# Attention with the row maxima first: how the first rows of maxima reach the queries, and where the last lead products stand

## The chip, the cores and the metric

The kernel runs on one core of one Trainium2 chip. Its engines work side by side and meet only at semaphores: TensorE (PE, with its weight loads PEld shown apart), VectorE (DVE), ScalarE (ACT), GpSimd (POOL) and the sync engine SP, which here only issues transfers. The metric is the device time of one execution in microseconds (us). Three runs of the kernel before took 1555.54, 1555.70 and 1554.82 us, median 1555.54.

## The reference

One transformer block on 2048 rows of 512 numbers: a modulated layer norm, attention with 32 query heads of 16 numbers on one shared key and value head, an output projection, a gate and a residual, then a second modulated layer norm and a two-layer network with gelu.

```
mod = (silu(c) @ w_mod)                     # six rows of 512: sa, ca, ga, sb, cb, gb
h = layernorm(x) * (1 + ca) + sa
q = (h @ wq), 32 heads of 16;  k = h @ wk;  v = h @ wv      # one k and one v for all heads
scores = q . k * 16 ** -0.5
p = softmax(scores);  o = p @ v;  x = x + ga * (o @ wo)
h = layernorm(x) * (1 + cb) + sb
x = x + gb * (gelu(h @ w1 + b1) @ w2 + b2)
```

## The kernel before

**Attention in units.** The 2048 rows are cut into eight blocks of 256, the 32 heads into eight groups of four: 64 units. A unit goes through two passes over all 2048 keys. The first takes maxima: a score product `m` (L512; 128 queries against 512 keys on one half of the array's rows) goes to a PSUM bank and VectorE reduces it to one maximum for each query (L517, `mx`). A unit has 32 such products, and 64 units have 2048. The second pass computes the scores again, now with keys as rows (`e`, L617), and ScalarE takes the exponential into SBUF (`p`, L621); then `acc` (L638) multiplies with the values.

**Where the maxima go.** A softmax needs the maximum subtracted before the exponential. The kernel lets the array do that: the operand tiles `qst` have two rows in each half, 48 and 49 (and 112 and 113), that hold the maximum's high and low part, against rows of `ks` that are -1. So no `e` of a unit can start before its maxima stand in those rows. The way there is `put_max`: VectorE reduces `mx` to `mm` (128 queries x 8) and turns it in 32x32 squares (`turned`), GpSimd gathers the four bands into `mt` (8 x 128, L560), splits that into a high and a low part `mh` and `ml` (L133, L140), and transfers write them into `qst` (L555), one for each part and half.

**The start.** Ahead of the loop over units stands a stretch with an order of its own, the table `SLOTS`: each entry takes a number of score products (`chunk`) and then names pieces of other work, such as the key projections ("keys"), the last query projection ("q 1", tile `qps`), turning the values into place ("v 2", "v 3", tile `vps`), preparing query weights ("wq"), and four pieces of modulation rows ("rows", tile `modl`). The score products in it belong to the units 0 and 1, alternately for the lower and upper half of the array. Their PSUM banks are a ring of three (tag `m`): a product can start when the product three before it in the ring has been reduced. PSUM has three more banks for exponentials (`e0` to `e2`), one for `x` and one for `v`.

**The lead.** After the table the score products must have reached a given count ahead of the exponentials, `lead[0]`, which is 56: all 32 of unit 0 and 24 of unit 1. Then `keep_warm` issues products whose result nobody reads, so that TensorE has work while the first rows travel. Then the loop begins. It goes in half steps, each ending with an `acc` group of eight products (16 in the profile's count); in a half step four `e` and, as a rule, four `m` are mixed, and in most of them a batch of other products (projections, the network) in between. The number of `m` in a step comes from `lead`, so a product that is not made before the loop is made in its first step. In the function `plain`, used for the first step, one `m` of each half step is put into bank `x`.

The order on each engine is exactly the order in which the program issues.

Of the kernel before, what the change touches and what calls it, by code (L numbers as in the profile page):

```python
# [8 lines left out]
F32 = mybir.dt.float32  # L9
# [5 lines left out]
P = 128  # L15
# [5 lines left out]

LEAD = 6
LEAD_0 = 6
FIRST_MAX = ((0, 0), (1, 0), (0, 1), (1, 1), (0, 2), (0, 3), (1, 2), (1, 3))
SLOTS = ((2, "keys 1", "keys 1"), (2, "keys 1", "keys 1"), (2, "low 1", "heads 2"), (2, "heads 2", "k 1"), (1, "warm"), (1, "heads 2"), (2, "heads 2", "v 0"),
# [4 lines left out]
MAX_WAIT = (1, 4)  # L30
QBUFS = 4
PREP = 4
# [9 lines left out]
SOON = 6  # L42
GROUP = 4
NORM_WAIT = 6
WARM = (4, 16, 2, 5)
MOD_WAIT = 3
AHEAD = 4.5

# [1 line left out]
def raw(ap):  # L50
    return ap.bitcast(F32)
# [3 lines left out]
def adaln_mqa_mlp(  # L55
# [15 lines left out]
    nc = tc.nc  # L71
# [22 lines left out]
    att = ctx.enter_context(tc.tile_pool(name="att", bufs=1))  # L94
    psum = ctx.enter_context(tc.tile_pool(name="psum", bufs=1, space=bass.MemoryType.PSUM))

    def pad(pool, nbytes, name):

        nc.gpsimd.memset(pool.tile([P, nbytes // 4], F32, name=name), 0.0)
# [27 lines left out]
    def ebank():  # L127
        turns[0] += 1
        return dict(tag=f"e{turns[0] % 3}", bufs=1)

    def split(dst_h, dst_l, src, eng_h, eng_l, between=None):
        if eng_h is nc.gpsimd:
            eng_h.tensor_scalar(out=dst_h, in0=src, scalar1=1.0, scalar2=0.0, op0=ALU.mult, op1=ALU.add)  # L133
        elif eng_h is nc.scalar:
            eng_h.copy(dst_h, src)
        else:
            eng_h.tensor_copy(out=dst_h, in_=src)
        if between:
            between()
        eng_l.tensor_tensor(out=dst_l, in0=src, in1=raw(dst_h), op=ALU.subtract)  # L140
# [7 lines left out]
    def later(n, fn):  # L148
        if draining[0]:
            fn()  # L150
        else:
            pending.append((clock[0] + n, fn))
# [130 lines left out]

    idles = []

    def keep_warm(n, **place):

        for k in range(n):
            if k == 0 or not place:
                ps = psum.tile([P, BQ], F32, name=f"idle{len(idles)}", **(place or dict(tag="m", bufs=3)))  # L290
                idles.append(ps)
            nc.tensor.matmul(ps, wkH[:, 0, :], wkH.rearrange("p k n -> p (k n)"), start=True, stop=True)

    def mod_rows(ps, k, wm):

# [19 lines left out]
    wkH = pro.tile([P, KD, P], F32R, name="wkH")  # L315
# [32 lines left out]
    bigH = att.tile([P, NB - 1, KD, BQ], F32R, name="bigH", tag="bigH")  # L348
# [8 lines left out]
    def stats1(b, between=None):  # L357
        mv, rs = ln_stats(xts[b], pro, QT, between)
        nm = pro.tile([P, QT], F32, name=f"nm{b}", tag="nm", bufs=2)
        if b:  # L360
            nc.gpsimd.tensor_tensor(out=nm, in0=mv[:, :, 0], in1=rs, op=ALU.mult)
            nc.gpsimd.tensor_scalar(out=nm, in0=nm, scalar1=-1.0, scalar2=0.0, op0=ALU.mult, op1=ALU.add)
        hts_stats[b] = mv, rs, nm

    def xhat1(b, eng):

        mv, rs, nm = hts_stats[b]
        xt = xts[b]
# [118 lines left out]
    class Max:  # L487


        def __init__(self):  # L490
            def products(u, kcs):
                return [(u, j, t, kc) for kc in kcs for j in range(2) for t in range(blocks[units[u][0]][1] // P)]

            def in_rows(u):
                return [(u, j, t, kc) for j in range(2) for t in range(blocks[units[u][0]][1] // P) for kc in range(NKC)]


            begin = [o for u, kc in FIRST_MAX for o in products(u, [kc])]
            self.todo = [begin + [o for u in range(2, NU) for o in in_rows(u)] for _ in range(2)]
# [30 lines left out]
    placed = set()  # L530
# [5 lines left out]
    def put_max(u, mx):  # L536

        T = blocks[units[u][0]][1] // P  # L540
        qst = qsts[u]
        mm = mms[u % 2]
        turned = att.tile([P, 32], F32, name=f"turned{u}", tag="turned", bufs=2)
        if u == 0:
            pad(att, 256, "pad7")
        mt = att.tile([4 * T, P], F32, name=f"mt{u}", tag="mt", bufs=2)
        mh = att.tile([4 * T, P], F32R, name=f"mh{u}", tag="mh", bufs=2)
        ml = att.tile([4 * T, P], F32R, name=f"ml{u}", tag="ml", bufs=2)

        def send():  # L550
            for s in range(2):
                for r, src in ((48, mh), (49, ml)):
                    dst = qst[64 * s + r:64 * s + r + 1].rearrange("p j (t n) -> p (j t) n", n=P)
                    ring = nc.scalar if u == 0 and s else nc.sync
                    ring.dma_start(out=raw(dst), in_=raw(src[2 * T * s:2 * T * (s + 1), :].unsqueeze(1)))  # L555
            placed.add(u)

        def gather():
            for g in range(0, P, 32):
                nc.gpsimd.tensor_scalar(out=mt[:, g:g + 32], in0=turned[g:g + 4 * T, :], scalar1=1.0, scalar2=0.0,  # L560
                                        op0=ALU.mult, op1=ALU.add)
            split(mh, ml, mt, nc.gpsimd, nc.gpsimd)

        def reduce():
            nc.vector.tensor_reduce(out=mm[:, :4 * T], in_=mx, axis=AX.X, op=ALU.max)
            nc.vector.transpose(out=turned, in_=mm)  # L566
            later(MAX_WAIT[0], gather)
            later(MAX_WAIT[1], send)


        if NQ <= u < NQ + 2:
            reduce()
        else:
            later((0 - clock[0]) % 4 + 1, reduce)
# [661 lines left out]
    first = [sum(size[:u]) for u in range(NU + 1)]  # L1236
    mp = Max()

    def chunk(n):
        for _ in range(n):  # L1240
            mp.step(mp.done % 2)

    act, dve, pool = nc.scalar, nc.vector, nc.gpsimd

# [50 lines left out]
    def warm():  # L1295
        keep_warm(WARM[2], tag="x")
        yield
# [16 lines left out]
    mod1(0, 0, act, pool)  # L1314
    turn1(0, 3)
    keep_warm(WARM[0])
    mod1(0, 1, pool, dve, lambda: stats1(1))
    load_constants()
    mod1(0, 2, act, dve)
    mod1(0, 3, act, dve)  # L1320
    rows = xhat1(1, act)
# [17 lines left out]
    def last_h(t):  # L1339
        if t == QT - 1:  # L1340
# [6 lines left out]
    run(xhat1(3, pool))  # L1347
    keep_warm(WARM[1])
    work = {"keys 1": keys(1), "heads 2": heads(2), "heads 3": heads(3), "q 1": q_group(), "keys 2": keys(2), "keys 3": keys(3),
            "v 0": one(v_out, 0), "v 1": one(v_out, 1), "v 2": one(v_out, 2), "v 3": one(v_out, 3), "rows": late_rows(),  # L1350
            "low 1": one(low_k, 1), "low 2": one(low_k, 2), "low 3": one(low_k, 3), "k 1": one(repeat_k, 1), "k 2": one(repeat_k, 2), "k 3": one(repeat_k, 3), "load": one(load_q, 2), "warm": warm(),
            "wq 1": one(prep_wq, 1), "wq 2": one(prep_wq, 2), "wq 3": one(prep_wq, 3)}
    for n, *names in SLOTS:
        chunk(n)
        for name in names:
            next(work[name])
    assert 0 in placed and len(mods_late) == KD
    draining[0] = False
    nc.gpsimd.tensor_scalar(out=b1r, in0=b1c, scalar1=GELU_R, scalar2=0.0, op0=ALU.mult, op1=ALU.add)
# [8 lines left out]
    lead = [first[u + 1] + 4 * LEAD for u in range(NU)] + [first[NU] + 4 * LEAD]  # L1368
    for u in range(NQ):
        lead[u] = min(first[1] + 4 * LEAD_0 + (lead[NQ] - first[1] - 4 * LEAD_0) * u / NQ, first[u + QBUFS - 1] - 2)  # L1370

# [1 line left out]

        return sum(b_.shape[-1] * (4 if b_.dtype == F32 else 1) for _, _, b_, _, _ in batch) / 512

    while mp.done < lead[0]:
        chunk(1)
    preps["w1"] = prep_w1()
    w2H = w2L = None
# [27 lines left out]
            if units[u][1] == NQ - 1:  # L1407
                put_off(rest(units[u][0], units[u][0] == len(blocks) - 1))

    keep_warm(WARM[3], tag="e2", bufs=1)  # L1410
    behind = None
    bare = [False]
    for u in range(NU):
        for K in range(0, steps[u], 2):
            goal = lead[u] + (lead[u + 1] - lead[u]) * (K + 2) / steps[u]
            goal = min(goal, first[u + QBUFS] if u + QBUFS < NU else first[NU])
            n = max(0, 2 * round((goal - mp.done) / 2))
# [165 lines left out]
```

## Time and profile before

| what | value |
|---|---|
| median of three runs | 1555.54 us |
| the profiled execution | 1555.99 us |
| its span, first to last instruction | 1554.1 us |
| PE busy | 1537.9 us (99%) |
| DVE busy | 1398.3 us (90%) |
| ACT busy | 1230.4 us (79%) |
| POOL busy | 683.7 us (44%) |
| score reductions on DVE, 2048 of them | 1270.6 us |

A timeline row gives the start, the duration, the engine, the source line, the operation, output and inputs, and how many instructions were merged into it; in brackets stands the idle time before and what ended it. The duration of a merged row runs from the first start to the last end. Matmul durations overlap, so the pace of TensorE is read from starts. A row of the chain of waits gives start, duration, and the work that the end of the program goes back to; "issue" is time in which the engine waited for nothing that the profile shows.

### The profile page before, as it was taken

What the parts mean: (1) busy time and instruction counts of PE and PEld (TensorE: products, weight loads), DVE (VectorE), ACT (ScalarE), POOL (GpSimd) and SP (SyncE); (2) the same over time, 40 slices, a digit from 0 to 9 for tenths busy, and PEclk for the clock granted to TensorE, in tenths of its full rate; (3) what the DMA queues carried; (4) which work ended last, traced back from release to release, by engine and by line L of the source; (5) the groups of instructions that cost most, each with busy time, mean ns of one, the idle gap of its engine ahead of it and who ended that gap; (6) DMA issues with size and microseconds to landing.
All of it is one profiled execution on the core that took longest, in us unless ns stands there. A gap on an engine that the chain in (4) does not pass through costs nothing.

```text
span 1554.1 us, 41556 instructions
## 1 busy us (share of the span) xinstructions
PE 1537.9 (99%) x16405; PEld 954.4 (61%) x16405; DVE 1398.3 (90%) x2488; ACT 1230.4 (79%) x2401; POOL 683.7 (44%) x1206
## 2 busy tenths in 40 slices
PE   7999999999999999999999999999999999999999
PEld 4455555567655665557655676556655676566658
DVE  7999999999999999999999999999999999999814
ACT  5577778788877887788877888788877888778874
POOL 5535432867422571246521563235711574046511
PEclk9999999999999999999999999999999999999999
DMA  7226412413030220303112120302212230203141
GB/s 240 102 89 199 151 57 81 130 51 97 18 105 26 72 68 28 103 19 109 33 51 79 56 87 16 111 26 88 68 30 73 60 101 25 87 28 99 48 150 48
DMA packets 84215, 120.85 MB, mean 78 GB/s; under 512 B 21342, under 2 KB 57438, under 8 KB 83764
## 3 DMA queue, kind: packets, MB, share of 16 engines
q1 hardware_dynamic: 84004, 118.18, 23.7%
q8 instruction: 130, 2.13, 0.6%
q14 instruction: 65, 0.53, 0.1%
q10 hardware_dynamic: 16, 0.00, 0.0%
HBM read 90.87 MB, written 26.74 MB: 76 GB/s over the span
## 4 chain that ended last, share of the span: by engine, by line
PE 86%; DVE 8%; issue 3%; POOL 2%; DMA 1%; ACT 0%; SPq 0%; POOLq 0%; DVEq 0%
PE acc L638 29%; PE m L512 23%; PE e L617 16%; PE w1ps L198 8%; DVE mx L517 6%; PE w2ps L198 2%; PE w2ps L188 2%; DMA xt<-in_A_x_dram 1%; PE w1ps L188 1%; PE wops L198 1%; PE tp L198 1%; PE qps L198 1%; PE kps L165 1%; DVE st L823 0%; DVE x L816 0%
## 5 line engine op out<-in xcount | busy, mean ns | idle before, releaser
L517 DVE TENSOR_REDUCE mx<-m 128x1 f32<-128x512 f32 x2048 | 1270.6, 682 | 86.6 <-PE m L512 65.1
L621 ACT ACTIVATE p<-e 128x512 f32<-128x512 f32 x2048 | 1098.8, 598 | 255.1 <-PE e L617 112.0
L512 PE MATMUL m<-ks,qst 64*128 64x512 f32 x2048 | 836.7, 429 | 2.0 <-DVE mx L517 0.6
L617 PE MATMUL e<-qst,ks 64*128 64x512 f32 x2048 | 740.2, 412 | 0.0
L638 PE MATMUL acc<-p,va 128*32 128x256 f32 x8192 | 548.0, 385 | 0.0
L512 PEld LDWEIGHTS m<-ks,qst 64*128 64x128 f32 x2048 | 368.2, 184 | 205.1 <-DVE mx L517 173.5
L617 PEld LDWEIGHTS e<-qst,ks 64*128 64x128 f32 x2048 | 359.6, 184 | 89.3 <-ACT p L621 62.5
L638 PEld LDWEIGHTS acc<-p,va 128*32 128x32 f32 x8192 | 214.0, 109 | 213.9 <-issue 110.9
L198 PE MATMUL w1ps<-h2H,w1t 64*128 64x256 f32 x1232 | 235.5, 287 | 0.0
L560 POOL TENSOR_SCALAR mt<-turned 8x32 f32<-8x32 f32 x256 | 53.1, 208 | 399.9 <-DVE turned L566 387.9
L198 PEld LDWEIGHTS w1ps<-h2H,w1t 64*128 64x128 f32 x1232 | 186.0, 185 | 28.9 <-DVE mx L517 14.8
L198 PE MATMUL w1ps<-h2L,w1t 64*128 64x256 f32 x616 | 169.3, 275 | 0.0
L198 PE MATMUL w2ps<-w2H,gH 64*128 64x512 f32 x274 | 120.3, 439 | 0.0
L198 PEld LDWEIGHTS w1ps<-h2L,w1t 64*128 64x128 f32 x616 | 114.1, 185 | 0.0
L198 PE MATMUL w2ps<-w2L,gH 64*128 64x512 f32 x274 | 107.5, 392 | 0.0
L198 PE MATMUL w2ps<-w2H,gL 64*128 64x512 f32 x274 | 106.9, 390 | 0.0
L975 POOL TENSOR_SCALAR tt<-tt 128x256 f32<-128x256 f32 x77 | 31.0, 402 | 131.5 <-ACT tt L974 96.5
L140 POOL TENSOR_TENSOR gL<-z,gH 128x256 fp32r<-128x256 f32 x77 | 57.0, 741 | 6.4
L976 POOL TENSOR_TENSOR tt<-tt,z 128x256 f32<-128x256 f32 x77 | 56.7, 736 | 6.4
L986 POOL TENSOR_TENSOR z<-tt,z 128x256 f32<-128x256 f32 x77 | 56.4, 732 | 6.0
L985 POOL TENSOR_TENSOR tt<-tt,z 128x256 f32<-128x256 f32 x77 | 56.5, 733 | 0.0
L198 PEld LDWEIGHTS w2ps<-w2H,gH 64*128 64x128 f32 x274 | 50.4, 184 | 6.7 <-DVE ot L1038 2.5
(193 smaller groups left out, 1503.5 us busy)
## 6 DMA issues: line engine op xcount, KB each, us to landing
w1t<-dw SPq DMA_DIRECT2D x82, 512.0 KB
qst<-dq SPq DMA_DIRECT2D x384, 32.0 KB
do<-oc SPq DMA_DIRECT2D x62, 128.0 KB
dw<-w1s SPq DMA_DIRECT2D x11, 512.0 KB
xt<-in_A_x_dram SPq DMA_DIRECT2D x4, 1024.0 KB
dq<-qH SPq DMA_DIRECT2D x16, 256.0 KB
dq<-qL SPq DMA_DIRECT2D x16, 256.0 KB
x<-in_A_x_dram SPq DMA_DIRECT2D x8, 512.0 KB
```

What stands on the lines that cost most here:

```text
L140: eng_l.tensor_tensor(out=dst_l, in0=src, in1=raw(dst_h), op=ALU.subtract)
L188: nc.tensor.matmul(ps, a, b_, start=first_, stop=last_)
L198: ins = nc.tensor.matmul(ps, a[rows], b_[rows], start=first_ and s == 0, stop=last_ and s == 1)
L512: nc.tensor.matmul(m, qsts[u][rows, j, t * P:(t + 1) * P], ks[rows, kc * 512:(kc + 1) * 512], start=True, stop=True)
L517: nc.vector.tensor_reduce(out=self.mx[u][:, i, kc:kc + 1], in_=m, axis=AX.X, op=ALU.max)
L560: nc.gpsimd.tensor_scalar(out=mt[:, g:g + 32], in0=turned[g:g + 4 * T, :], scalar1=1.0, scalar2=0.0, op0=ALU.mult, op1=ALU.add)
L617: nc.tensor.matmul(e, ks[rows, kt * P:(kt + 1) * P], rhs, start=True, stop=True)
L621: ins = nc.scalar.activation(dst, e, AF.Exp, scale=0.25)
L638: ins = nc.tensor.matmul(accs[u][32 * cidx:32 * cidx + 32, :], va[:, kt, :], rhs, start=kt == 0, stop=kt == NKT - 1)
L976: nc.gpsimd.tensor_tensor(out=tt, in0=tt, in1=z, op=ALU.mult)
L985: nc.gpsimd.tensor_tensor(out=tt, in0=tt, in1=z, op=ALU.mult)
L986: nc.gpsimd.tensor_tensor(out=z, in0=tt, in1=z, op=ALU.add)
```

## The change

For unit 0 alone the maxima take another way: VectorE turns `mm` in four squares straight into `mt`, and splits it too; each of the two parts is one transfer from SP that writes both halves' rows. Before, GpSimd gathered and split, and SP and ScalarE issued two transfers each. Four lead products, which stood before the loop, are made in the loop's first step instead. In the table the pieces move: "v 2" and all four "rows" come later, "wq 2" and "wq 3" come earlier. One lead product of the table gets a bank of the exponentials instead of the ring. The five unread products become two, with another operand and in bank `v`.

```diff
+LEFT = 4
 SLOTS = (...
-         (2, "low 2", "k 2", "v 1", "wq 1"), (0, "keys 3"), (2, "keys 3"), (2, "keys 3"), (2, "keys 3"), (2, "low 3", "k 3"),
-         (0, "v 2"), (2, "q 1"), (2, "q 1"), (2, "q 1"),
-         (2, "q 1", "rows"), (2, "v 3", "wq 2"), (2, "rows"), (2, "rows"), (2, "rows", "wq 3", "load"))
+         (2, "low 2", "k 2", "v 1", "wq 1"), (0, "keys 3"), (2, "keys 3"), (2, "keys 3"), (2, "keys 3"), (2, "low 3", "k 3", "wq 2", "wq 3"),
+         (2, "q 1"), (2, "q 1"), (2, "q 1"),
+         (2, "q 1"), (2, "v 2"), (2, "v 3", "rows"), (2, "rows"), (2, "rows"), ("rows", "load"))
...
-WARM = (4, 16, 2, 5)
+WARM = (4, 16, 2, 2)
...
-            nc.tensor.matmul(ps, wkH[:, 0, :], wkH.rearrange("p k n -> p (k n)"), start=True, stop=True)
+            nc.tensor.matmul(ps, src[:, :P], src, start=True, stop=True)
...
-        mt = att.tile([4 * T, P], F32, name=f"mt{u}", tag="mt", bufs=2)
+        mt = att.tile([4 * T if u else 32, P], F32, name=f"mt{u}", tag="mt", bufs=2)
...
-                    ring = nc.scalar if u == 0 and s else nc.sync
-                    ring.dma_start(out=raw(dst), in_=raw(src[2 * T * s:2 * T * (s + 1), :].unsqueeze(1)))
+                    nc.sync.dma_start(out=raw(dst), in_=raw(src[2 * T * s:2 * T * (s + 1), :].unsqueeze(1)))
+            placed.add(u)
+
+        def place_first():
+            for g in range(0, P, 32):
+                nc.vector.transpose(out=mt[:, g:g + 32], in_=mm[g:g + 32, :])
+
+            def send_row(r, src):
+                dst = qst[r:r + 65:64].rearrange("p j (t n) -> p (j t) n", n=P)
+                nc.sync.dma_start(out=raw(dst), in_=raw(src.unsqueeze(1)))
+
+            split(mh, ml, mt[:4 * T], nc.vector, nc.vector, lambda: send_row(48, mh))
+            send_row(49, ml)
             placed.add(u)
...
             nc.vector.tensor_reduce(out=mm[:, :4 * T], in_=mx, axis=AX.X, op=ALU.max)
+            if u == 0:
+                place_first()
+                return
...
-            mp.step(mp.done % 2)
+            mp.step(mp.done % 2, **(ebank() if wide[0] and mp.done % 2 else {}))
...
-    while mp.done < lead[0]:
+    while mp.done < lead[0] - LEFT:
...
-    keep_warm(WARM[3], tag="e2", bufs=1)
+    keep_warm(WARM[3], bigH[:, 0, 0, :], tag="v")
```

TensorE between the lead products and the first `acc`, before: `m_u`'s four numbers are half of the queries, 128-row piece, 512-key piece and array half (`m_1_1_2_1` on `qst_158` is unit 1's); `e_0_1_0` is key step, half step and array half.

```order
L512 MATMUL m_1_0_2_0_879<-ks,qst_158 128x512
L512 MATMUL m_1_0_2_1_882<-ks,qst_158 128x512
L512 MATMUL m_1_1_2_0_885<-ks,qst_158 128x512
L512 MATMUL m_1_1_2_1_888<-ks,qst_158 128x512
L292 MATMUL idle_891<-wkH 128x512 x5
L617 MATMUL e_0_0_1_898<-qst_157,ks 128x512
L617 MATMUL e_0_0_0_901<-qst_157,ks 128x512
L512 MATMUL m_0_0_3_1_904<-ks,qst_158 128x512
```

And the same place in the kernel after.

```order
L299 MATMUL modl<-wml_439,csb 32x512 x4
L299 MATMUL modl<-wml_578,csb 32x512 x4
L294 MATMUL idle_876<-bigH 128x512 x2
L633 MATMUL e_0_0_1_880<-qst_157,ks 128x512
L633 MATMUL e_0_0_0_883<-qst_157,ks 128x512
L514 MATMUL m_1_0_2_1_886<-ks,qst_158 128x512
L514 MATMUL m_1_0_2_0_889<-ks,qst_158 128x512
L633 MATMUL e_0_1_1_892<-qst_157,ks 128x512
L514 MATMUL m_1_1_2_0_895<-ks,qst_158 128x512
L514 MATMUL m_1_1_2_1_898<-ks,qst_158 128x512
```

The two pairs of `m` that stood ahead of the unread products now stand behind the first `e`, so that the first step holds twelve `m` and not eight; the last two pieces of `modl` took their place.

The end of the first step, before:

```order
L617 MATMUL e_1_1_1_935<-qst_157,ks 128x512
L512 MATMUL m_1_1_3_0_938<-ks,qst_158 128x512
L512 MATMUL m_1_1_3_1_941<-ks,qst_158 128x512
L617 MATMUL e_1_1_0_948<-qst_157,ks 128x512
L638 MATMUL acc_951<-p_897,va 32x256 x8
```

The end of the first step, after:

```order
L633 MATMUL e_1_1_1_923<-qst_157,ks 128x512
L514 MATMUL m_1_0_3_0_926<-ks,qst_158 128x512
L514 MATMUL m_1_0_3_1_929<-ks,qst_158 128x512
L514 MATMUL m_1_1_3_0_932<-ks,qst_158 128x512
L514 MATMUL m_1_1_3_1_935<-ks,qst_158 128x512
L633 MATMUL e_1_1_0_942<-qst_157,ks 128x512
L654 MATMUL acc_945<-p_879,va 32x256 x8
```

In both the last `m` before the first `acc` is unit 1's last; four `m` and not two stand between the last two `e`. From this `acc` on TensorE has the same order in both kernels.

VectorE where unit 0's maxima are complete, before:

```order
L517 TENSOR_REDUCE mx_482<-m_1_1_3_1_817 128x1
L565 TENSOR_REDUCE mm_192<-mx_482 128x8
L566 STREAM_TRANSPOSE turned_820<-mm_192 128x32
L517 TENSOR_REDUCE mx_544<-m_0_0_2_0_842 128x1
L517 TENSOR_REDUCE mx_544<-m_0_0_2_1_845 128x1
```

And after:

```order
L519 TENSOR_REDUCE mx_482<-m_1_1_3_1_810 128x1
L578 TENSOR_REDUCE mm_192<-mx_482 128x8
L561 STREAM_TRANSPOSE mt_816<-mm_192 32x32 x4
L138 CAST mh_817<-mt_816 8x128
L141 TENSOR_TENSOR ml_818<-mt_816,mh_817 8x128
L519 TENSOR_REDUCE mx_544<-m_0_0_2_0_839 128x1
L519 TENSOR_REDUCE mx_544<-m_0_0_2_1_842 128x1
```

Four turns, a cast and a subtraction stand where one turn stood.

More of the change, by code (lines that the diff above doesn't have):

```diff
@@ L284, in adaln_mqa_mlp, with keep_warm @@
     idles = []
-    def keep_warm(n, **place):
+    def keep_warm(n, src=None, **place):
+        src = wkH.rearrange("p k n -> p (k n)") if src is None else src
         for k in range(n):
@@ L1237, in adaln_mqa_mlp @@
     mp = Max()
+    wide = [False]
     def chunk(n):
         for _ in range(n):
-            mp.step(mp.done % 2)
+            mp.step(mp.done % 2, **(ebank() if wide[0] and mp.done % 2 else {}))
     act, dve, pool = nc.scalar, nc.vector, nc.gpsimd
@@ L1352, in adaln_mqa_mlp @@
             "wq 1": one(prep_wq, 1), "wq 2": one(prep_wq, 2), "wq 3": one(prep_wq, 3)}
[L1353 to L1356, printed above, removed]
+    for i, slot in enumerate(SLOTS):
+        wide[0] = i == len(SLOTS) - 3
+        for part in slot:
+            if isinstance(part, int):
+                chunk(part)
+            else:
+                next(work[part])
     assert 0 in placed and len(mods_late) == KD
```

## The prediction

> **What bounds the kernel now.** I read the page first, then the chain of waits over the end of the prologue, then the timelines of the engines there. The page says that the program's end goes back mostly to TensorE.
>
> ```profile
> span 1554.1 us, 41556 instructions
> PE 86%; DVE 8%; issue 3%; POOL 2%; DMA 1%; ACT 0%; SPq 0%; POOLq 0%; DVEq 0%
> ```
>
> The instructions behind the first `acc` stand in one order in both kernels, so the change can only move the moment of that `acc`. This is the chain of waits around it:
>
> ```profile
> 72.59 0.69 DVE mx L517
> ...
> 73.82 1.40 PE idle L292 x5
> ...
> 75.91 2.50 DVE mx L517 x4
> 78.45 0.49 PE m L512
> 78.95 1.00 PE acc L638 x16
> ...
> 81.93 1.00 PE acc L638 x16
> ...
> 84.77 1.00 PE acc L638 x16
> ```
>
> The first step (75 to 79 us) is paced by VectorE: four score reductions, then the `m` that waited for its bank, then `acc`. The gap to the second `acc` is 2.98 us, the next 2.84. Behind the first two half steps TensorE sets the pace, as VectorE's rows confirm, and a delay of the first `acc` stays in the time to the end:
>
> ```profile
> 60.77 5.22 DVE L517 TENSOR_REDUCE mx<-m 128x1 f32<-128x512 f32 x8
> 67.05 2.48 DVE L517 TENSOR_REDUCE mx<-m 128x1 f32<-128x512 f32 x4 [1.05 <-PE m L512]
> 69.56 0.19 DVE L565 TENSOR_REDUCE mm<-mx 128x8 f32<-128x32 f32 x1
> 69.78 0.21 DVE L566 STREAM_TRANSPOSE turned<-mm 128x32 f32<-128x32 f32 x1
> 69.92 5.14 DVE L517 TENSOR_REDUCE mx<-m 128x1 f32<-128x512 f32 x8
> 75.91 7.27 DVE L517 TENSOR_REDUCE mx<-m 128x1 f32<-128x512 f32 x12 [0.85 <-PE m L512]
> 86.23 2.48 DVE L517 TENSOR_REDUCE mx<-m 128x1 f32<-128x512 f32 x4 [0.35 <-PE m L512]
> ```
>
> In the loop it reduces four products in 2.48 us and then idles 0.35 us; between 60 and 76 us it idles only twice, 1.05 and 0.85 us. Where it works without a gap, twelve reductions take 7.27 us, 0.606 each.
>
> **The change part by part.** I follow one clock through the place, from 65.5 us to the second `acc`.
>
> ```profile
> 65.51 1.06 PE L297 MATMUL modl<-wml,csb 128*32 128x512 f32 x8
> 66.94 0.43 PE L419 MATMUL vps<-ident,vt 32*128 32x32 f32 x4
> 67.30 0.98 PE L512 MATMUL m<-ks,qst 64*128 64x512 f32 x2
> 67.79 0.18 PEld L512 LDWEIGHTS m<-ks,qst 64*128 64x128 f32 x1 [0.30 <-DVE mx L517]
> 68.21 0.16 PEld L297 LDWEIGHTS modl<-wml,csb 128*32 128x32 f32 x8 [0.24 <-issue]
> 69.21 0.49 PE L512 MATMUL m<-ks,qst 64*128 64x512 f32 x2
> 73.75 1.47 PE L292 MATMUL idle<-wkH 128*128 128x512 f32 x5
> 75.14 0.49 PE L617 MATMUL e<-qst,ks 64*128 64x512 f32 x2
> 78.44 0.18 PEld L512 LDWEIGHTS m<-ks,qst 64*128 64x128 f32 x1 [0.36 <-DVE mx L517]
> 78.88 1.07 PE L638 MATMUL acc<-p,va 128*32 128x256 f32 x16
> ```
>
> *Pieces moved.* A `modl` piece stood at 65.51 and kept VectorE waiting 1.05 us. Now the next pair of `m` starts there. Its bank is free: of the eight reductions from 60.77 on, the last ends at 65.99. So reductions go on at 65.51 + 0.50 = 66.01, 1.04 us earlier than 67.05. "v 2" taken from its old place (near 58.6 us) gives nothing, since the next `m` there waits for VectorE anyway. "v 2" now costs 0.36 (66.94 to 67.30), while the last `m` of unit 0 waits for its bank: that `m` started 0.74 after the reductions did (67.05 to 67.79), so now at 66.75. The weight pieces moved on ScalarE and GpSimd fall into idle time of both: GpSimd does not wait on the path there, and its last piece is done before the query part needs it.
>
> *The first `e`.* From 66.75 TensorE has: the `m` 0.42 (67.79 to 68.21), "v 3" 0.36, a `modl` piece 1.00 (68.21 to 69.21), a pair of `m` 0.42, `modl` 1.00, a pair 0.42, two `modl` 2.00, two unread products. Five took 1.39 (73.75 to 75.14); at 0.23 each, a fifth of what lies between, rounded down for the wait at their end, two take 0.69. The sum is 6.31, and the first `e` stands at 73.06 instead of 75.14: 2.08 us earlier. No row shows two `modl` pieces back to back; the wait of 0.24 ahead of the second may fall away, or not, so 0.76 to 1.00; I take 1.00, as the rows have it. The banks are free: the `m` in a bank of the exponentials is the second of four that are reduced by 72.4 (below).
>
> *VectorE's new work.* Reductions of unit 0 end at 66.01 + 2.48 = 68.49 and `mm` starts at 68.52. The turns: one took 0.14 from start to start (69.78 to 69.92) and 0.21 to its end. I take 0.14 for each of four smaller ones and 0.07 more for the last (0.24 each, if each is waited for). Nearest rows for the cast and the subtraction, and the rows of the transfers:
>
> ```profile
> 13.33 0.36 DVE L329 TENSOR_TENSOR wkL<-wkv,wkH 128x192 fp32r<-128x192 f32 x1
> 13.60 0.19 DVE L328 CAST wkH<-wkv 128x64 fp32r<-128x64 f32 x1
> ...
> 68.29 0.33 SPq L424 DMA_DIRECT2D dq<-qL  x1
> 71.50 0.69 SPq L555 DMA_DIRECT2D qst<-mh  x1
> 72.29 0.61 SPq L555 DMA_DIRECT2D qst<-ml  x1
> 72.96 0.59 ACTq L555 DMA_DIRECT2D qst<-ml  x1
> 75.29 0.59 ACT L1364 COPY modl_sb<-modl 128x512 f32<-128x512 f32 x1 [0.96 <-ACT wqH L342]
> ```
>
> A cast of 128 columns lies above the 0.19 of 64 columns and below 0.36; I take 0.22, and 0.30 for the subtraction. `mh` is there at 68.74 + 0.56 + 0.07 + 0.22 and two gaps of 0.03, so 69.65; reductions go on at 69.85, or 1.33 us after `mm` began where it was 0.36 (69.56 to 69.92). The 0.97 more lie in idle time: four reductions end at 72.33, and the next product comes only behind the first `e`. Without that cover they would go straight into the first `acc`.
>
> *Two transfers.* SP is free (its `dq<-qL` at 68.29 is the one ahead). `mh` is issued at 69.65, `ml` 0.79 later (71.50 to 72.29), at 70.44. Landing is in no row; the bound is the last of the four before: issued at 72.96, landed by 75.14 at the latest, 2.18. So it is there by 72.62, 0.44 us before TensorE wants it; from below it is 70.44 plus the 0.61 of issuing. Either way TensorE's own queue sets the first `e`, and what VectorE saved over GpSimd is worth only that it stays hidden. The six loads of the third unit's queries follow on SP about 1.9 us earlier. ScalarE loses its two transfers; its copy of `modl` now comes right behind the last `modl` piece, near 73, beside the first `e`, and frees bank `x` about when the second `m` wants it.
>
> *Four products in the first step.* This is the cost. The first reduction of the step starts 0.77 after the first `e` (75.14 to 75.91): at 73.83. Twelve `m` stand before the first `acc`, and two of them are in bank `x`. So the ring's last one waits for the product three before it in the ring, the ninth of the step; before, it waited for the fourth of eight (75.91 + 2.50, then 78.44: the rule fits). Nine take 5.45, end 79.28, the `m` starts 0.04 later, and `acc` 0.44 after that (78.44 to 78.88): 79.76 against 78.88, **0.88 later**. What was gained at the first `e` (2.08) is less than the five more reductions that stand before `acc` (5 x 0.606 = 3.03, less rounding). At that point VectorE has three reductions left in both kernels, and its queue is level with TensorE's when the next `m` comes, 1.0 us later; so the second gap should be 2.84 and not 2.98, 0.14 back.
>
> Sum: +0.88 - 0.14 = **+0.74 us**. Against the profiled execution (1555.99: span 1554.1 and 1.89 around it) that is 1556.7; that execution lies 0.45 above the median of the runs, so against the median 1555.54 I say **1556.3**. Own range of this case: 0.3 to 1.3 later, and the spread of the three runs, so 1555.5 to 1557.2. A change of 0.2%, 3.1 us, is about what a measurement of this kernel can tell from none, so this is no change.
>
> **The rivals.** *A: the gain at the first `e` is kept.* If the deferred maxima cost nothing, because VectorE's idle time in the loop takes them up, the time is 1555.54 - 2.08 - 0.14, about 1553.3. For it: 0.35 us of idle time in each half step. Against it: the order puts all twelve ahead of the first `acc`.
>
> *B: the rows still come late.* If the two transfers, each with twice the rows, land so late that the first `e` stays at 75.14, the longer first step is paid in full: 2.08 + 0.74, so 1558.4. It decides for slower from a first `e` after 75.4 on. For it: no row shows a landing. Against it: the bound above.
>
> *C: TensorE's clock falls.* The first step now has 20 products in 6.7 us, where 16 had 3.74, and three unread products less before it. The table by stage shows the granted clock there and in the loop:
>
> ```profile
> 75.10:78.90 3.80, 3.69 (x21) 1.65 (x20) 2.99 (x5) 3.61 (x8) 0.65 (x2) 1.00 0.17 43
> 81.90:84.70 2.80, 2.80 (x31) 1.68 (x30) 2.77 (x8) 2.10 (x4) 0.84 (x5) 1.00 0.03 6
> ```
>
> It is 1.00 in both (the seventh figure, behind five engines' busy times). If it halved, each half step of 2.84 would take up to twice as long: one costs 2.84, so 1559.1 and slower; two 1562. One is the point from which it decides. The longest gap by my sum is that between the ring's last two products, about 1.2 us (two reductions). The Trainium skill, "TensorE: Matmul & The Clock Gate", section "Why this matters for your kernels", warns of gaps above some 3 us, after which the clock is at half; that rule speaks against a thinner first step, but by it a gap of 1.2 us leaves the clock up, and the granted clock here has shown nothing else. So I give it little.
>
> **How the numbers follow.** My sum 0.64, A 0.18, B 0.12, C 0.06. Of A, 0.04 lies beyond -3.1 us, with whatever I don't see; of B, 0.03 beyond +3.1; C lies there whole. So faster 0.04, slower 0.09, same 0.87. The range reaches to A and B: 1553.3 to 1558.5.
>
> **What would show it.** In the changed profile: the reductions' idle of 1.05 us before the last four of unit 0 is gone; four turns, a cast and a subtraction take about 1.3 us with `mm`; the first `e` stands near 73.1 and waits for no transfer; VectorE then idles about 1.5 us before the step's first reduction; the chain shows nine reductions, not four, ahead of the first `acc`, which stands near 79.8; the next comes 2.84 later. I am wrong if the first `e` is held by a transfer, if the first `acc` comes before 78.9, or if the gaps behind 82 us differ from before.

## The result, and the profile after

Six runs of the changed kernel took 1565.58 to 1568.81 us, median 1567.35; six of the kernel before beside them 1554.82 to 1557.62, median 1555.76. The ratio is 1.0073 (95% interval 1.0060 to 1.0086): 11.6 us slower, far outside the forecast range. The profiled execution took 1567.40. One of the eleven runs of experiment 12 below took 1619.67 us at a mean granted clock of 0.886, and its ratio leaves that run out.

Its page has these lines: the span, the granted TensorE clock over 40 slices of 39 us, and the chain's share by engine.

```profile
span 1565.6 us, 41542 instructions
PEclk9799999999999999999999999999999999999999
PE 90%; DVE 7%; DMA 1%; ACT 1%; POOL 0%; issue 0%; SPq 0%; DVEq 0%
```

The loss lies in the second slice (39 to 78 us), where the clock digit is 7, and shortly behind it. All start times below are counted from one event that both kernels have ahead of the change, the last split of the keys on VectorE (`ks<-kps,ks`: at 60.06 us before, 59.78 after); I call it S. Before, the first three `acc` start 18.82, 21.80 and 24.64 us behind S, after 28.47, 33.40 and 36.23. The third is 11.59 us later, and the medians differ by 11.59: everything is lost ahead of it.

The timeline of the kernel after, from S on (start, duration, engine, line, operation; in brackets the idle time before and its releaser):

```profile
59.78 0.68 DVE L409 TENSOR_TENSOR ks<-kps,ks 16x512 fp32r<-16x512 f32 x1
...
61.14 1.34 ACT L344 CAST wqH<-wqf 128x256 fp32r<-128x256 f32 x4
61.24 0.49 PE L514 MATMUL m<-ks,qst 64*128 64x512 f32 x1 [0.27 <-DVE mx L519]
61.63 2.81 POOL L345 TENSOR_TENSOR wqL<-wqf,wqH 128x256 fp32r<-128x256 f32 x4 [4.32 <-ACT wqH L344]
62.53 0.79 PE L166 MATMUL qps<-h0H,wqH 128*128 128x512 f32 x1 [0.79 <-ACT wqH L344]
64.50 0.80 PE L166 MATMUL qps<-h0H,wqL 128*128 128x512 f32 x1 [1.18 <-POOL wqL L345]
```

The query products `qps` of "q 1" (head group 1) now wait 0.79 us for ScalarE and 1.18 us for GpSimd, for the very pieces that moved, "wq 2" and "wq 3". Those prepare the weights of groups 2 and 3, of which this product reads nothing.

The windows of TensorE in the same kernel (length, busy time with its instructions, granted clock, DMA share, GB/s) show what came of it:

```profile
60.00:62.00 2.00, 1.46 (x5) 1.00 0.03 8
62.00:64.00 2.00, 0.79 (x1) 0.53 0.00 0
64.00:66.00 2.00, 1.50 (x4) 0.50 0.00 0
...
76.00:78.00 2.00, 2.00 (x10) 0.50 0.07 18
78.00:80.00 2.00, 2.00 (x14) 0.70 0.19 50
80.00:82.00 2.00, 2.00 (x16) 1.00 0.13 34
82.00:84.00 2.00, 0.98 (x6) 1.00 0.00 0
84.00:86.00 2.00, 1.80 (x9) 1.00 0.00 0
86.00:88.00 2.00, 1.56 (x4) 0.51 0.00 0
...
90.00:92.00 2.00, 2.00 (x14) 0.50 0.00 0
92.00:94.00 2.00, 2.00 (x24) 0.79 0.00 0
```

The clock is at half from 62 to about 79 us, recovers, and falls again near 86, at the end of the first step of the loop. In the kernel before it is 1.00 in every window from 60 us on. At half clock a `qps` product takes 0.79 us instead of 0.50. The chain of waits goes through both places:

```profile
61.63 2.82 POOL wqL L345 x4
64.50 1.22 PE qps L166 x2
...
81.30 0.42 PE e L633
81.72 0.28 PE m L514 x2
82.01 5.47 DVE mx L519 x9
87.52 0.79 PE m L514
88.32 1.86 PE acc L654 x16
...
93.25 1.00 PE acc L654 x16
```

The first `acc` group takes 1.86 us instead of 1.00, and the second comes 4.93 us behind it instead of 2.98.

### The profile page after: what moved, and what is told of

Its sections match the earlier page's. It is cut to its first block, busy times and chain, and to the rows that moved or that the text cites. A ratio compares the mean times of both kernels' runs of the same rounds, so it can differ in the third digit from the quotient of the medians.

```text
span 1565.6 us, 41542 instructions
## 1 busy us (share of the span) xinstructions
PE 1546.1 (99%) x16402; PEld 955.5 (61%) x16402; DVE 1399.6 (89%) x2493; ACT 1231.6 (79%) x2401; POOL 683.8 (44%) x1200
## 4 chain that ended last, share of the span: by engine, by line
PE 90%; DVE 7%; DMA 1%; ACT 1%; POOL 0%; issue 0%; SPq 0%; DVEq 0%
PE acc L654 30%; PE m L514 25%; PE e L633 17%; PE w1ps L199 8%; DVE mx L519 6%; PE w2ps L199 2%; PE w2ps L189 2%; PE qps L199 1%; DMA xt<-in_A_x_dram 1%; PE w1ps L189 1%; PE tp L199 1%; PE wops L199 1%; PE kps L166 1%; DVE st L839 0%; PE modl L299 0%; DVE x L832 0%
```

## The experiments

Two theories stood for the two falls. **W**: the early weight pieces stall TensorE, and the stall costs the clock. **D**: the four deferred products make the first step thin, and that alone costs the clock there. A rival to W, **V**: "v 2", which moved away from just ahead of "q 1", had kept TensorE busy there. A rival to D: the second fall is an after-effect of the first.

The table has each kernel's median, its ratio to the kernel before on the same chip, and from its profile the start of the first `acc` behind S and the gap from there to the second. A profile is one execution; its shift differs from that of the medians by up to 1.3 us.

| kernel | median us | ratio (95%) | first `acc` | gap |
|---|---|---|---|---|
| before | 1555.76 | 1 | 18.82 | 2.98 |
| after | 1567.35 | 1.0073 (1.0060–1.0086) | 28.47 | 4.93 |
| 1: after, weight pieces back | 1559.96 | 1.0025 (1.0015–1.0034) | 19.88 | 4.57 |
| 2: before, weight pieces early | 1561.29 | 1.0031 (1.0019–1.0043) | 24.88 | 2.97 |
| 3: after, "v 2" back | 1566.57 | 1.0064 (1.0048–1.0081) | 28.12 | 4.78 |
| 4: after, unread products over the wait | 1563.34 | 1.0044 (1.0029–1.0059) | 22.69 | 4.92 |
| 5: 1 without the deferral | 1556.42 | 1.0000 (0.9991–1.0009) | 18.41 | 3.00 |
| 6: 1 with a large filler in the first step | 1560.63 | 1.0034 (1.0023–1.0045) | 22.37 | 2.85 |
| 7: after, weights stored by group | 1559.88 | 1.0031 (1.0019–1.0043) | 19.62 | 4.41 |
| 8: before with the deferral alone | 1561.51 | 1.0032 (1.0020–1.0045) | 21.41 | 4.54 |
| 9: 1 with a small filler in the first step | 1558.16 | 1.0008 (0.9999–1.0017) | 19.98 | 2.85 |
| 10: before, value and row pieces later | 1556.79 | 0.9998 (0.9990–1.0007) | 19.02 | 2.99 |
| 11: before, turn and split on VectorE | 1558.90 | 1.0012 (1.0003–1.0021) | 20.36 | 2.99 |
| 12: 7 without the deferral | 1556.36 | 0.9999 (0.9990–1.0009) | 18.30 | 2.98 |

Every timed run also has its mean granted clock, so that the falls need not be read from one execution alone. It lies below 1.000 in all six runs of the kernel after (0.992 to 0.995) and in every run of 1, 2, 3, 4, 7 and 8, and at 1.000 in every run of 9, 10 and 11. It is not always so clean: the kernel before has 0.997 to 0.999 in 10 of its 77 runs beside the experiments, which took 1557.44 to 1559.81 us; 5 has one run at 0.997 and 6 one at 0.996; and in 7 two of the six runs lie at 0.993 and 0.997 (1565.01 and 1562.26 us), the others at 0.998 and 0.999.

**1. The weight pieces put back behind "q 1".**

```diff
-         ... (2, "low 3", "k 3", "wq 2", "wq 3"),
+         ... (2, "low 3", "k 3"),
-         (2, "q 1"), (2, "v 2"), (2, "v 3", "rows"), (2, "rows"), (2, "rows"), ("rows", "load"))
+         (2, "q 1"), (2, "v 2"), (2, "v 3", "rows", "wq 2"), (2, "rows"), (2, "rows"), ("rows", "wq 3", "load"))
```

> The changed kernel with one thing undone: "wq 2" goes back behind all of "q 1" (with "v 3"), "wq 3" to the last entry. Theory W (the weight pieces put ahead of "q 1" make TensorE wait some 0.8 + 1.2 us for ScalarE and GpSimd at 61.7 to 64.5 us, and the clock falls there): no wait at 62 us, granted clock 1.00 up to the first step, first acc near 79.8; 1556.3 if the thin first step keeps the clock, 1559 to 1563 if the clock falls a second time there by itself. Theory V (the clock falls because "v 2" left its place near 58.6, and TensorE has less work in the window before 62): the clock still falls at 62 and the time stays near 1567.

The stall and the first fall are gone; 8.6 us of the first `acc`'s delay go with them. 3.6 us over the kernel before remain. The windows show the second fall all the same, so it is no after-effect of the first:

```profile
74.00:76.00 2.00, 1.30 (x7) 1.00 0.16 49
76.00:78.00 2.00, 1.88 (x6) 0.61 0.00 0
78.00:80.00 2.00, 1.60 (x11) 0.50 0.00 0
```

**2. The early weight pieces alone, in the kernel before.**

```diff
-         ... (2, "low 3", "k 3"),
+         ... (2, "low 3", "k 3", "wq 2", "wq 3"),
-         (2, "q 1", "rows"), (2, "v 3", "wq 2"), (2, "rows"), (2, "rows"), (2, "rows", "wq 3", "load"))
+         (2, "q 1", "rows"), (2, "v 3"), (2, "rows"), (2, "rows"), (2, "rows", "load"))
```

> The kernel before with only the weight pieces moved: "wq 2" and "wq 3" stand with "k 3", ahead of "q 1". Theory W: the wait of 0.8 + 1.2 us appears near 62 and the clock falls to half for 10 us or more; no second fall, since the first step has eight maxima; 1561 to 1565. Theory V: "v 2" is in its old place, the clock stays 1.00, and only the wait is paid, at most 2 us: 1556 to 1558.

The two waits are there as in the kernel after (0.80 and 1.18 us), and the clock is at half from 62 to 72 us. It does not fall a second time, and the gap stays 2.97. The early pieces are enough by themselves for the first fall, and for 6.1 us at the first `acc`.

**3. "v 2" back ahead of "q 1".**

```diff
-         (2, "q 1"), (2, "q 1"), (2, "q 1"),
-         (2, "q 1"), (2, "v 2"), (2, "v 3", "rows"), ...
+         (0, "v 2"), (2, "q 1"), (2, "q 1"), (2, "q 1"),
+         (2, "q 1"), (2,), (2, "v 3", "rows"), ...
```

> The changed kernel with only "v 2" put back to its old place ahead of "q 1"; the weight pieces stay early. Theory W: the wait and both falls stay, 1565 to 1568. Theory V: no fall at 62; the wait alone costs, 1557 to 1562 with or without a fall in the first step.

Both waits and both falls stay; the time is within the interval of the kernel after. V falls. But these rows also show something that W has wrong:

```profile
60.83 0.49 PE L514 MATMUL m<-ks,qst 64*128 64x512 f32 x1
61.59 0.62 PE L514 MATMUL m<-ks,qst 64*128 64x512 f32 x1 [0.27 <-DVE mx L519]
62.88 0.79 PE L166 MATMUL qps<-h0H,wqH 128*128 128x512 f32 x1 [0.67 <-ACT wqH L344]
```

The granted clock is at half from 61.80 us on, and the `m` at 61.59 already takes 0.62 us and not 0.50. The wait for the weight piece only begins at 62.21, and up to there TensorE has had the same products at the same pace as in the kernel before. In the kernel after the fall stands at 62.13, 0.4 us into the first wait. So the stretch ahead of the wait counts, and the wait of 1.18 us behind it can't have started the fall. What starts it stays open. That it belongs to the early pieces rests on the runs: the mean granted clock is 0.992 to 0.996 in every run of the kernel after and 3, and 0.998 in every run of 1, where the pieces are back.

**4. Twelve unread products where TensorE waited.** They stand just ahead of the second slice of "q 1" (`fill`, bank `x`).

```diff
-         (2, "q 1"), (2, "q 1"), (2, "q 1"),
+         (2, "q 1"), (2, "fill", "q 1"), (2, "q 1"),
...
+    def fill():
+        keep_warm(12, tag="x")
+        yield
```

> The changed kernel with twelve unread products (2.8 us at full clock) on TensorE just ahead of the second "q 1" piece, where it waits for the weight pieces. If the clock is the cost and not the wait: granted clock 1.00 at 62 to 80 us though the array does nothing more that is read; the time is that of e1_wq_back plus 2 to 3 us. If the wait itself, passed on through the maxima, is the cost: no better than 1567.

The fill runs for 3.07 us and `qps` follows it without idle time. The clock stays 1.00 to 79.9 us; then it falls in the first step as in the kernel after:

```profile
76.00:78.00 2.00, 0.99 (x6) 1.00 0.16 49
78.00:80.00 2.00, 1.80 (x9) 0.99 0.07 16
80.00:82.00 2.00, 1.57 (x4) 0.50 0.00 0
```

The first `acc` stands 2.81 us behind that of experiment 1 and 5.78 ahead of the kernel after. So of the delay that the weight pieces bring, about a third is the wait (here spent on unread products) and two thirds the clock.

**5. Experiment 1 without the deferral.**

```diff
-LEFT = 4
+LEFT = 0
```

> e1_wq_back with LEFT = 0: the four lead products are made ahead of the loop again, the first step has eight maxima. Theory D (the deferral thins the first step and the clock falls there): granted clock 1.00 throughout; VectorE has no gap of 1.05 us any more, the first acc comes at about 77.8 (before: 78.88), and the time is 1 to 1.5 us under the kernel before. Rival (the clock falls because only two unread products stand before the first e, or because the place of the rows moved): a fall near 77 us here too, and about 1559.

The time is that of the kernel before, the clock 1.00 throughout; the 1 to 1.5 us that I expected to gain did not come. VectorE reduces without a gap from the first product after the split to beyond the second `acc`:

```profile
69.38 0.70 DVE L141 TENSOR_TENSOR ml<-mt,mh 8x128 fp32r<-8x128 f32 x1
70.02 12.24 DVE L519 TENSOR_REDUCE mx<-m 128x1 f32<-128x512 f32 x20
77.95 1.07 PE L654 MATMUL acc<-p,va 128*32 128x256 f32 x16
80.95 1.07 PE L654 MATMUL acc<-p,va 128*32 128x256 f32 x16
```

So the 3.6 us that remained in experiment 1 came with the deferral.

**6 and 9. The clock in the first step held up by unread products.** To experiment 1, behind ten of the step's twelve `m`, one unread product is added. In 6 it uses the whole array; in 9 it has 64 rows and uses the half of the array that the step's own products use at that moment.

```diff
+                def with_fill(fn):
+                    fn()
+                    keep_warm(1, bigH[:, 0, 0, :], tag="v")
...
+                if u == 0 and not behind:
+                    one, other = filled(one), filled(other[:-1]) + other[-1:]
```

and for 9, in place of `keep_warm`:

```diff
...
+                    rows = slice(64 * half_, 64 * half_ + 64)
+                    nc.tensor.matmul(ps, qsts[1][rows, 0, 0:P], ks[rows, 0:512], start=True, stop=True)
```

> e1_wq_back with one unread product behind ten of the twelve maxima of the first step, in the bank of the values, so that TensorE is never thin while VectorE paces it. If the clock made the difference between 1556.3 (forecast, at full clock) and e1_wq_back: granted clock 1.00, gap from the first to the second acc 2.8 to 3.0 us instead of 4.57, time 1.5 to 2.5 us under e1_wq_back and within 1 us of the forecast's +0.7 over before. If VectorE's longer step is the cost: no better than e1_wq_back.

> The first repair again (both weight pieces back behind the query slices), and behind ten of the twelve maxima of the thin first step one small unread product, of 64 rows and in the half of the array that the step's own products use. If what is left over the kernel before is the clock that falls in the thin step: clock 1.00 through the step, the first value product 19.4 to 20.4 us behind the last split of the keys, the second about 2.85 us behind it instead of 4.57, and 1.2 to 2.0 us less than the first repair: about the time before +1.5 to +3.0 us. If filling costs as much as the clock, because the maxima then wait for TensorE (as with the large filler): the first value product 21 us or more behind that split, and no better than the first repair. If the clock falls all the same: the gap stays above 4 us.

In 6 the clock is 1.00 and the gap 2.85, but the whole-array products stand 0.86 us apart and VectorE waits for the `m` between them, as in these rows:

```profile
75.15 0.50 PE L294 MATMUL idle<-bigH 128*128 128x512 f32 x1
75.26 0.69 DVE L519 TENSOR_REDUCE mx<-m 128x1 f32<-128x512 f32 x1 [0.16 <-PE m L514]
76.02 0.50 PE L294 MATMUL idle<-bigH 128*128 128x512 f32 x1
```

The first `acc` comes at 22.37, so this run shows that the clock can be held, but not what its fall costs. Experiment 9 does:

```profile
73.36 7.27 DVE L519 TENSOR_REDUCE mx<-m 128x1 f32<-128x512 f32 x12 [0.70 <-PE m L514]
78.89 0.49 PE L514 MATMUL m<-ks,qst 64*128 64x512 f32 x1 [0.50 <-DVE mx L519]
79.68 1.07 PE L654 MATMUL acc<-p,va 128*32 128x256 f32 x16
...
82.53 1.07 PE L654 MATMUL acc<-p,va 128*32 128x256 f32 x16
```

Here twelve reductions run without a gap, the first `acc` is 0.10 us from where experiment 1 has it, its group takes 1.07 us, and the second follows 2.85 us later instead of 4.57. Each against its own runs of the kernel before, experiment 1 is 3.62 us slower and experiment 9 is 1.51 (ratio 0.9999 to 1.0017, so 1.51 is hardly told from none): the second fall costs about 2 us by the medians, and 1.62 by the second `acc` of the two profiles. The rest, +1.16 at the first `acc`, is the longer first step.

**7. The query weights stored group after group.** Everything stands where the change put it; only the order of the columns in `wqH` and `wqL` differs, so that a group's 512 numbers of a partition lie together instead of in four pieces between those of the other groups.

```diff
-    wqH = att.tile([P, KD, D], F32R, name="wqH", tag="gH")
-    wqL = att.tile([P, KD, D], F32R, name="wqL", tag="gL")
+    wqH = att.tile([P, KD, KD, P], F32R, name="wqH", tag="gH")
+    wqL = att.tile([P, KD, KD, P], F32R, name="wqL", tag="gL")
...
-        return [(wqH[:, k, gs], wqL[:, k, gs], hH[:, k, :], hL[:, k, :]) for k in range(KD)]
+        return [(wqH[:, g, k, :], wqL[:, g, k, :], hH[:, k, :], hL[:, k, :]) for k in range(KD)]
```

> The changed kernel, but the split query weights lie by groups of heads, so that the pieces of groups 2 and 3 touch no address between the first and the last that the product of group 1 reads; the pieces stay early. If TensorE waited at 62 us for pieces that its product does not read: that wait and the first fall of the clock are gone, the second stays, and the time is that of e1_wq_back (3 to 4 us over before). If the wait is a need of the product, or of the engines' queues: 1567 as the changed kernel.

The pieces run as early as in the kernel after, and the products beside them:

```profile
61.45 1.34 ACT L344 CAST wqH<-wqf 128x256 fp32r<-128x256 f32 x4
61.55 0.50 PE L513 MATMUL m<-ks,qst 64*128 64x512 f32 x1 [0.28 <-DVE mx L518]
61.94 2.85 POOL L345 TENSOR_TENSOR wqL<-wqf,wqH 128x256 fp32r<-128x256 f32 x4 [4.34 <-ACT wqH L344]
61.98 0.50 PE L166 MATMUL qps<-h0H,wqH 128*128 128x512 f32 x1
62.31 0.39 PE L166 MATMUL qps<-h0H,wqL 128*128 128x512 f32 x1
```

The stall was no shortage of an engine or a port: it was an order between a product and writes that it doesn't read, and it went when their addresses no longer interleaved. With it the first fall went from the profile; two of the six runs lost more of the clock than the profiled one, and no trace shows where. The second fall stays (gap 4.41), as in 1 and 8. For that fall the trace gives one more number, the list of TensorE's waits between 72 and 82 us (total, times, longest):

```profile
PE m L513 <- DVE mx L518: 1.7, 3, 0.7
```

In this step the clock fell with no wait longer than 0.7 us.

**8. The deferral alone, in the kernel before.**

```diff
+LEFT = 4
-         ... (2, "rows"), (2, "rows"), (2, "rows", "wq 3", "load"))
+         ... (2, "rows"), (0, "rows"), (0, "rows", "wq 3", "load"))
-    while mp.done < lead[0]:
+    while mp.done < lead[0] - LEFT:
```

> The kernel before with only the four lead products moved into the loop's first step; GpSimd still gathers and splits, the weight pieces and the values stay in place. Theory D: the first step has twelve maxima and is paced by VectorE for 7.3 us, the clock falls to half in it and recovers in the next half step; 3 to 6 us over before. Without a fall of the clock: at most 3 us (five more reductions before the first acc).

D by itself makes the second fall: the clock is at half from 79 to 86 us, the gap 4.54. The first `acc` is 2.59 us later. The first `e` comes only 0.70 us earlier (14.38 us behind S, against 12.87 in experiment 1): TensorE has less ahead of it, but now it waits 0.39 us for a transfer of `ml`.

**10. The order of the value and row pieces alone, in the kernel before** (the weight pieces no earlier than there).

```diff
-         (0, "v 2"), (2, "q 1"), (2, "q 1"), (2, "q 1"),
-         (2, "q 1", "rows"), (2, "v 3", "wq 2"), (2, "rows"), (2, "rows"), (2, "rows", "wq 3", "load"))
+         (2, "q 1"), (2, "q 1"), (2, "q 1"),
+         (2, "q 1"), (2, "v 2"), (2, "v 3", "rows", "wq 2"), (2, "rows"), (2, "rows"), (0, "rows", "wq 3", "load"))
```

> The kernel before, with nothing changed but the order of its pieces: the value piece two slots before the next, the row pieces behind that, both weight pieces where the kernel before has them or later, all lead products still ahead of the first exponential, and GpSimd still turns the maxima. If the order of the pieces is harmless apart from the weight pieces: clock 1.00, no stall at the query products, and the time before within 1 us; VectorE's pause of about 1 us before its last reductions may go, for a first value product up to 1 us earlier (18.82 us behind the last split of the keys in the kernel before). If the value or row pieces, too, delay something on the path: first value product later than 19.3 us, and +0.5 us or more.

**11. Turn, split and two transfers alone** (`place_first`, in the kernel before).

```diff
+            if u == 0:
+                place_first()
+                return
```

> The kernel before, with only the first rows of maxima turned in four squares and split on VectorE and sent in two transfers; the four lead products stay ahead of the first exponential, and all pieces stay where they are. VectorE takes on 0.84 + 0.21 + 0.28 us for a turn and GpSimd's work in the kernel before. If the reductions ahead of the first exponential bind VectorE, as the forecast has it: first value product later by up to 1 us, +0.3 to +1.0 us. If the transfers of the rows bound it instead: 0 to -0.5 us. Clock 1.00 in either case, since the four products stay where they fill TensorE.

The order of those pieces alone is worth nothing. VectorE's pause of 1.05 us ahead of unit 0's last reductions does go, but one of 1.00 us appears four reductions further on, where the kernel before has none, and the first `acc` is at 19.02. The turn and split on VectorE alone cost: the first `acc` is 1.54 us later and the time 2.2 us longer. The rows show the pause still there and the new work behind it:

```profile
67.54 2.48 DVE L517 TENSOR_REDUCE mx<-m 128x1 f32<-128x512 f32 x4 [1.04 <-PE m L512]
...
70.28 0.84 DVE L560 STREAM_TRANSPOSE mt<-mm 32x32 f32<-32x32 f32 x4
71.16 0.57 DVE L137 CAST mh<-mt 8x128 fp32r<-8x128 f32 x1
71.76 0.30 DVE L140 TENSOR_TENSOR ml<-mt,mh 8x128 fp32r<-8x128 f32 x1
```

Together, in experiment 5, the two cost nothing, with the first `acc` 0.41 us earlier than before. The likely reading is that the reductions that start sooner pay for VectorE's new work; no run shows it by itself, since experiment 5 also has two unread products, 0.66 us, where the kernel before has five, 1.39 us.

**12. Both causes taken away:** the storage of experiment 7 and `LEFT = 0`, every piece where the change put it.

> The changed kernel with both causes taken away and every piece where the change put it: the query weight's tiles stored group after group, and the four lead products ahead of the first exponential again (LEFT = 0). If the stall and the thin step are the whole loss: no wait at the query products, clock 1.00 throughout, the second value product 2.98 us behind the first, and no split of the maxima beside a weight piece of GpSimd, so a subtraction of 0.28 us and a first value product 18.0 to 18.5 us behind the last split of the keys (18.82 in the kernel before): the time before -0.8 to +0.3 us. If the early weight pieces cost something besides the stall, the first value product comes later than 19 us behind that split, and the time is +0.7 us or more.

The clock is 1.00 throughout, and the first `acc` stands at 18.30, 0.52 us earlier than before. In the time this is not to be seen: the ratio is 0.9999, interval 0.9990 to 1.0009. No version tried beats the kernel before by more than its measurement is uncertain.

## Why the prediction was wrong

**The step that failed** is this sentence of the part on moved pieces: "The weight pieces moved on ScalarE and GpSimd fall into idle time of both: GpSimd does not wait on the path there, and its last piece is done before the query part needs it." The engines were idle there, but I asked only when the data of groups 2 and 3 are needed. "q 1" stands in between: its products read the same two tiles, and in the kernel after they wait for the writes issued ahead of them. The term set to zero measured this: the second product of that slice starts 4.72 us behind S in the kernel after and 2.22 in experiment 7, so 2.50 us of stall; and at half clock from there to the first `e` another 5.95, by difference (the first `e` is 21.45 behind S, against 13.00 forecast: 8.45, less 2.50). Experiment 4, which fills the wait and keeps the clock, agrees: its first `acc` is 5.78 earlier.

**Rival C was the other mistake.** I gave the thin first step a chance of 0.06 of losing the clock. It lost it in every kernel that had the deferral and no filler in that step: after, 1, 3, 4, 7 and 8. I had argued from the longest gap, about 1.2 us by my sum, and from the rule in the Trainium skill, "TensorE: Matmul & The Clock Gate", section "Why this matters for your kernels", that gaps above some 3 us bring the clock to half. The traces don't agree with that rule as a limit: with no wait over 0.7 us the clock fell in experiment 7, and 0.4 us into a wait of 0.79 us in the kernel after. The same page of the Trainium skill, section "A second HAM failure mode: psum-queue depth-cycling", tells of a clock that comes and goes because TensorE idles often and briefly; that is nearer to what experiments 1, 7 and 8 show, and I had not weighed it. C's price was nearly right: one half step at half clock was put at 2.84 us, and experiments 1 and 9 differ by about 2. That is partly luck: in experiment 1 the clock was down for 6.83 us, and for the first 4 us of that VectorE's reductions went on at their full rate.

**The rest came out as forecast, where those two don't hide it.** Counted from S:

- First `e`: forecast 13.00; 12.87 in experiment 1 and 12.88 in 7. The pieces do move as the order said, and no transfer holds the first `e`: the chain enters it from TensorE's own queue.
- VectorE's new work: forecast 1.33 us from `mm` to the next reduction. It is 1.55 in experiment 7: the four turns take 0.84, not 0.63; cast and subtraction 0.21 and 0.28 against 0.22 and 0.30. In experiment 1, where the subtraction takes 0.71, it is 1.98. It lies in idle time, as said: VectorE then idles 1.14 us ahead of the first step in 7 and 0.70 in 1. That it would go "straight into the first `acc`" without that cover is what experiment 11 shows: 1.93 us there against 0.36 in the kernel before, and the first `acc` 1.54 later.
- Nine reductions ahead of the first `acc`: the chain has `mx` x9 in 5.47 us, forecast 5.45. First `acc`: forecast 19.70; 19.62 in 7, 19.88 in 1, 19.98 in 9.
- Second gap: forecast 2.84; 2.85 in experiment 9, where the clock holds. In the kernel after it is 4.93.

The pieces add up: 0.74 forecast, 2.50 of stall, 5.95 of half clock, 0.32 more from the first `e` to the first `acc` (7.02 against 6.70), and 2.09 in the second gap make 11.60, against 11.59 measured. Rival A (the gain kept) is excluded by the chain's nine reductions, rival B (rows late) by the first `e` of experiments 1 and 7.

## What to carry to other kernels

A piece that prepares data may be moved ahead only after asking which waiting instructions touch the same tile, also parts of it that they don't read; if the parts interleave, store them apart and the wait goes. A stretch that another engine paces is not free for TensorE even when it lies in a few microseconds: read the granted clock window by window there, and of several runs, and price its fall as a case of its own. If such a stretch must be filled, try products that use the same half of the array as their neighbours: here those cost nothing that the rows show, and products of the whole array did.

## What the runs showed of the hardware

- TensorE's granted clock changed in steps. In the stretches looked at here each time at half clock is a multiple of 3.41 us: 17.07 and 6.83 us in the kernel after and in experiment 3, 10.24 in 2, 6.83 in 1, 4 and 8, 3.41 in 7; so is the time at full clock between the two falls, 6.83. Where the steps lie is not tied to the work: counted back from the falls, one starts 0.21 us ahead of S in 1, 1.06 in the kernel after, 1.74 in 3 and 2.17 in 8. That may be why a kernel loses the clock in some of its runs only; no run shows it.
- What decides at the end of a step stays open, but it is not TensorE's busy time in that step alone. Of 3.41 us the step ahead of a fall had 2.51 busy in the kernel after (from 58.72), 2.27 in 1 (from 73.03), 2.28 in 8 (from 75.66) and even 3.15 in 3 (from 58.39); steps with 2.29 in 11 (from 71.63, counted back from the fall at its end at 1556.43; a wait of 1.09 us lies in it), 2.38 in 7 (from 72.94) and 2.47 in 8 (from 72.25) kept 1.00. How much of the array its products use was not tried by itself.
- Once down, the clock can stay down although TensorE is busy: in the kernel after four whole steps, 65.55 to 79.20 us, have no idle time and are at half.
- Whole-array products between products of one half stood 0.86 us apart (experiment 6), where a half-array filler let twelve reductions run at their full rate (experiment 9).
- A short operation of VectorE can wait for GpSimd's. In experiment 11 the cast took 0.57 us and ended 0.08 us behind the weight piece that GpSimd was at; in the other kernels with `place_first` it took 0.21. GpSimd's row there:

```profile
70.91 0.74 POOL L343 TENSOR_TENSOR wqL<-wqf,wqH 128x256 fp32r<-128x256 f32 x1
```

  The subtraction took 0.70 to 0.71 us in experiments 1, 5 and 9, each time beside such a piece, and 0.28 in 7 and 12, where GpSimd's pieces were over. The Trainium skill, "SBUF — State Buffer", section "Who interferes with whom", has VectorE and GpSimd take a common pair of ports in turn, each for a whole instruction; these rows agree. On the first `acc` little comes of it: 5 and 12, which differ in this and in the place and storage of the weight pieces, have it 0.11 us apart (18.41 and 18.30).
